# Adding a step's outputs onto its queries' products in PSUM, in a fused DeltaNet and feed-forward kernel

## The chip, the cores and the metric

The kernel runs on one core of a Trainium2 chip. The metric is the device time of one execution in microseconds. Before the change it is 647.7 us, the median of three runs (647.32, 647.70 and 648.19).

Engine names in the profile: PE is TensorE's matmuls and PEld its weight loads, DVE is VectorE, ACT is ScalarE, POOL is GpSimd, and SP is SyncE, which issues most of the DMAs. PSUM is the memory that TensorE writes to. Here it is used as eight banks of 512 floats in each of 128 partitions.

## The reference, cut to what matters

Two blocks follow each other. The first is a delta rule over 768 tokens, for 4 batches of 8 heads of 48 dimensions:

```python
for t in range(S):
    y[:, :, t] = einsum('bhd,bhde->bhe', q[:, :, t], state)
    v_old = einsum('bhde,bhd->bhe', state, kt)
    state = state + bt * einsum('bhd,bhe->bhde', kt, vt - v_old)
```

Its output, 3072 tokens of 384 features, goes through a feed-forward network (FFN): `h = x @ w_in` (2048 wide), `g = max(h, 0) + alpha * min(h, 0)`, `g @ w_out`.

## The kernel before, in words

**Chunks and steps.** The tokens are cut into 12 chunks of 64. A chunk is worked on in two steps, one for each pair of batches, so there are 24 steps (0 to 23), and step n works on the state of pair n mod 2. Inside a step the recurrence is written as matrix products, always for 16 heads, as `quarters()` (L482) lists them. Each of them is a small matmul on a quarter of the array (64 x 64 cells), and shows as two matmuls in the profile:

- `grams` (L495): products of the keys with each other, needed eight or nine steps ahead. VectorE weighs and moves them out in two pieces (`same` and `right`, L507); a third piece, `keep` (L544), copies a part on.
- `through_state` (L790): keys times the state and keys times the queries. VectorE subtracts the first from the values (`r`, L809) and masks the second into `a_t` (L521).
- `solve` (L821): the inverse of the chunk's triangular matrix times `r`. VectorE weighs it into `u` (L828).
- `query` (L778): queries times the state, the share of the output that comes from earlier chunks. ScalarE copies it to `y` (L788).
- `outputs` (L833): `a_t` times `u`, the share from the chunk itself. VectorE adds it to `y` (L843).
- `next_state` (L847): keys times `u`. VectorE subtracts it from the state (L861).
- `between` (L749): 32 x 32 blocks of the inverse of the next steps, copied out by ScalarE (L745).

`to_ffn` (L869) transposes `y` on TensorE; ScalarE copies that to `xt`, the FFN's input. `turn_q` (L462) is a stream transpose of the raw queries on VectorE (L466). It writes them beside the state of their pair, in the place that `query` and `through_state` of that step read, and step n + 2 uses the same place. `load_q` (L175) loads the raw queries on SP's queue, into two buffers in turn.

**Order.** All engines follow the order of the program text, which is written by hand; the framework only adds the semaphores. From step 6 (`JOINED`) a step is three stretches (L1856 to L1898). A stretch begins with a piece of attention on TensorE and goes on with 8 to 18 parts of the FFN of earlier chunks, among which the `later` pieces, the elimination on VectorE (`eliminate`) and the placing of blocks on ScalarE are woven in equal distances (`weave`, L1328).

1. `burst_a(n)` (L1374): `outputs` and `next_state` of step n - 1, `through_state` of step n, and at once all that moves them out.
2. `turn_round(n)` (L1411): `to_ffn` of step n - 1, then as later pieces the transposes of keys and queries for steps to come (`turn_q(n + 2)`), the weights, and `load_q(n + 3)`.
3. `burst_b(n)` (L1395): `solve(n)`, `grams(n + 9)`, `query(n + 1)` from step 8 on (`NARROW`), and `between`. The moving out of all of these follows in the order u, block copies, y, Gram products. From step 16 (`LATE`) only u is moved out at once, and the rest later in the stretch. Gram products end with step 14.

**PSUM.** Up to step 7 there are three pairs of banks for attention and two single banks for the FFN; from step 8 on two pairs and four single ones (`banks(2, 2)`, L1858). `ps_big()` (L77) hands out the pairs in turn. In `burst_b` the solve and the blocks lie in one pair (`b`), the Gram products and the queries' products in the other (`x`): per bank 256 columns of the one and 192 of the other. In `burst_a` outputs and the state's products lie in one pair and `through_state` in the other.

**The FFN.** Up to chunk 7 `ffn_in` (L957; L966 matmuls, L976 on ScalarE and L978 on VectorE) and `ffn_out_fast` (L1019; L1031 matmuls) work chunk by chunk. The latter multiplies in a scheme of seven products that needs sums of operands, which VectorE makes just before (`operand_sums`, L920). From chunk 8 on `ffn_in_fast` (L1153) and `ffn_out_faster` (L1258; L1283 matmuls) run. There ScalarE copies one bank (L1218), GpSimd adds in SBUF (L1223), VectorE adds another bank (L1228) and applies the slope (L1237); the times of these are due times counted in parts (`Due`, L1119).

Of the kernel before, what the change touches and what calls it, by code (L numbers as in the profile page):

```python
# [32 lines left out]
C = 64  # L33
# [3 lines left out]
EARLY = 8  # L37
FIRST = 6
NARROW = 8
# [5 lines left out]
def kernel(  # L45
# [20 lines left out]
    G = H // 2  # L66
# [10 lines left out]
    def ps_big():  # L77

        big.append(big.pop(0))
        return big[-1]  # L80
# [24 lines left out]
    def half(i):  # L105
        return slice(64 * i, 64 * i + 64)

    def dims(i):
        return slice(64 * i, 64 * i + D)
# [5 lines left out]
    N = len(steps)  # L115
# [240 lines left out]
    state = [x[:, :, :, 0:D] for x in beside]  # L356
# [15 lines left out]
    stats, k_t, q_t, a_t = {}, {}, {}, {}  # L372
# [112 lines left out]
    def now(pieces):  # L485
        for x in pieces:
            x()
# [7 lines left out]
    def grams(n, p=None):  # L495

        if n >= N:
            return []
        p = region(p, G * C, g=G)
        for g, a, t in quarters():  # L500
            nc.tensor.matmul(
                p[half(t), a, g], k_t[n][dims(a), g, half(t)], k_t[n][dims(a), g, half(t)]
            )

        def weighted(dst, cols):
            w = stats[n][1][:, 0:2, :, None].to_broadcast([128, 2, G, HB])
            nc.vector.tensor_tensor(  # L507
                out=dst.rearrange("p (a g) i -> p a g i", a=2), in0=p[:, :, :, cols], in1=w,
                op=ALU.mult,
            )  # L510

        return [
            lambda: weighted(gather(n), slice(0, HB)),
            lambda: weighted(right[n % EARLY][:, 1:], slice(HB, C)),
            lambda: keep(n),
        ]
# [251 lines left out]
    nv, rhs_, ys, us, xts, whole = {}, {}, {}, {}, {}, set()  # L768
# [9 lines left out]
    def query(n, p=None):  # L778
        if n >= N:
            return []  # L780
        bp = steps[n][1]
        p = region(p, G * D, g=G)
        for g, a, t in quarters():
            nc.tensor.matmul(
                p[half(t), a, g], q_t[n][dims(a), t, g], state[bp][dims(a), t, g]
            )
        ys[n] = work.tile([128, H, D], FP32, name="y")
        return [lambda: nc.scalar.copy(by_parity(ys[n]), p)]  # L788

# [31 lines left out]
    def solve(n, p=None):  # L821
        p = region(p, G * D, g=G)
        for g, a, t in quarters():
            nc.tensor.matmul(  # L824
                p[half(t ^ a), a, g], inv[n % NE][half(t), a * G + g], rhs_[n][half(t), a, g]
            )
        us[n] = work.tile([128, 2, G, D], FP32, name="u")
        return [lambda: nc.vector.tensor_tensor(  # L828
            out=us[n], in0=p,
            in1=stats[n][1][:, 0:3:2, :, None].to_broadcast([128, 2, G, D]), op=ALU.mult,  # L830
        )]

    def outputs(n, p=None):  # L833
        c, bp = steps[n]
        p = region(p, G * D, g=G)
        for g, a, t in quarters():
            nc.tensor.matmul(  # L837
                p[half(t), a, g], a_t[n][half(t ^ a), a * G + g], us[n][half(t ^ a), a, g]
            )
        if c == 0:  # L840
            ys[n] = work.tile([128, H, D], FP32, name="y")
            return [lambda: nc.scalar.copy(by_parity(ys[n]), p)]
        return [lambda: nc.vector.tensor_tensor(  # L843
            out=by_parity(ys[n]), in0=by_parity(ys[n]), in1=p, op=ALU.add
        )]

    def next_state(n, p=None):  # L847
        c, bp = steps[n]
        pieces, wide = [], n < 2 * NJ
        if c < NCH - 1:  # L850
            p = region(p, G * D, g=G)
            for g, a, t in quarters():
                nc.tensor.matmul(
                    p[half(a) if wide else dims(a), t, g], k_late[n % NKL][half(t ^ a), 2 * g + a, 0 : C if wide else D],
                    us[n][half(t ^ a), a, g],
                )


            def less(rows):
                x = state[bp][rows]  # L860
                nc.vector.tensor_tensor(out=x, in0=x, in1=p[rows], op=ALU.subtract)  # L861

            if wide:
                pieces = [lambda: less(slice(0, 2 * C))]
            else:
                pieces = [lambda: less(dims(0)), lambda: less(dims(1))]
        return pieces
# [503 lines left out]

    WY, JOINED = G * D, NJ + 2

    def burst_a(n):  # L1374

        soon, later = [], []
        b = ps_big()
        if n > JOINED:
            soon += outputs(n - 1, b[:, :, 0:WY])
            soon += next_state(n - 1, b[:, :, WY : 2 * WY])  # L1380
            later.append(lambda: load_late(n + 1))
        if n < N:
            p = ps_big()
            y = ps_big()[:, :, 0:WY] if n < NARROW else None
            soon += through_state(n, p[:, :, 0 : G * (D + C)], y)
            if n < JOINED + 2:
                soon += between_1(n + 1, b[:, :, 2 * WY : 2 * WY + G * HB])
            if n == JOINED:
                soon += grams(n + EARLY, big[-1][:, :, WY : WY + G * C])
                later.append(lambda: squares(n + EARLY + 1))  # L1390
            later.append(lambda: load_v(n + 3))
        now(soon)
        return later

    def burst_b(n):  # L1395

        b, x = ps_big(), ps_big()
        soon = solve(n, b[:, :, 0:WY])
        gram = grams(n + EARLY + 1, x[:, :, 0 : G * C])
        asked = query(n + 1, x[:, :, G * C : G * C + WY]) if n + 1 >= NARROW else []  # L1400
        wanted = [(n + 1, True, b[:, :, WY : WY + G * HB])]
        if n > JOINED:
            wanted.append((n + 2, False, b[:, :, 2 * WY : 2 * WY + G * HB]))
        soon += between(*wanted)
        if n >= LATE:
            now(soon[:1])
            return soon[1:] + asked
        now(soon + asked + gram[:2])
        return gram[2:] + [lambda: squares(n + EARLY + 2), lambda: load_early(n + EARLY + 3)]

    def turn_round(n):  # L1411

        if n > JOINED:
            to_ffn(n - 1)
        if n == JOINED:
            flips(n + EARLY + 1, N)
            load_keys(steps[TURNED_K][0])
        later = []
        if TURNED_K <= n + EARLY + 1 < N:
            later.append(lambda: turn_k(n + EARLY + 1))  # L1420
        if n + 2 < N:
            later.append(lambda: turn_q(n + 2))
        later += weigh(n + EARLY + 1)
        return later + [lambda: load_q(n + 3)]
# [120 lines left out]
    n = 2 * W_IN_P  # L1545
# [111 lines left out]
    n = 12  # L1657
# [198 lines left out]
    for n in range(JOINED, N):  # L1856
        if n == NARROW:
            banks(2, 2)  # L1858
        fill, share = FILL.get(n, FILLS[n % 2]), PIECES_OF.get(n, TURNS[n % NJ])
        extra = [[], [], []]  # L1860
        if n == JOINED:
            place(n + 1, (0,))
            extra[1] = [(weight_sums(1, 0, 3), 3)]
            extra[2] = [(weight_sums(0, 3, 4), 1)]
        elif n == JOINED + 1:
            extra[0] = [(weight_sums(1, 3, 4), 1, 0.6), (placing(n + 1, (1, 2, 3)), PLACING)]

        later = burst_a(n)
        stretch(fill[0], blocks, share[0], later, *extra[0], *put_off)
        put_off = []  # L1870
        later = turn_round(n)
        if n == JOINED:
            extra[1].append((placing(n + 1, (1, 2, 3)), PLACING))
        stretch(fill[1], blocks, share[1], later, *extra[1], soon=0.2)
        m, ends = (n + 6) // NJ, n % NJ == 2
        if ends and n > JOINED:
            for _ in blocks:
                assert False
            place(n + 2, (0,))
        later = burst_b(n) + [lambda: scale_v(n + 1)]  # L1880
        if n == JOINED:
            stretch(fill[2], blocks, share[2], later, *extra[2])
            for _ in blocks:
                assert False
            place(n + 2, (0,))
            place(n + 3, (0,))
            blocks = eliminate(m)
        else:
            if ends:
                blocks = eliminate(m) if m < N // NJ else iter(())  # L1890
            after = [(placing(n + 2, (1, 2, 3)), PLACING)]
            if n % NJ != 1:
                after.append((placing(n + 3, (0,)), 1))
            if n >= LATE:
                put_off, after = after, []
            stretch(
                fill[2], blocks, share[2], later, *after, *extra[2], soon=0.1 if n >= LATE else 0.5
            )  # L1898
# [34 lines left out]
```

## Time and profile before

| | us |
|---|---|
| median of three runs | 647.7 |
| the profiled execution, in all | 647.16 |
| its span, first to last instruction | 645.4 |
| PE busy | 630.1 |
| VectorE busy | 502.9 |
| ScalarE busy | 253.0 |
| GpSimd busy | 94.0 |

Below is the time of each engine from about one burst B to the next, six times: from those of steps 9 and 10, of steps 16 and 17, and of steps 20 and 21 on. Each row gives the length, then the busy time of PE, PEld, VectorE, ScalarE and GpSimd, each with its count of instructions, and then the granted clock of TensorE, the share of DMA and its rate in GB/s.

```profile
253.00:279.00 26.00, 25.60 (x384) 24.39 (x383) 21.22 (x56) 6.17 (x17) 0.74 (x4) 1.00 0.20 37
279.00:302.00 23.00, 23.00 (x345) 19.82 (x343) 17.89 (x44) 9.80 (x24) 2.11 (x5) 1.00 0.42 65
...
424.00:446.00 22.00, 22.00 (x311) 19.17 (x307) 18.60 (x47) 7.90 (x18) 0.00 (x0) 1.00 0.27 40
446.00:471.00 25.00, 25.00 (x359) 24.16 (x357) 22.68 (x53) 4.62 (x12) 0.00 (x0) 1.00 0.14 30
...
517.00:538.00 21.00, 21.00 (x354) 19.83 (x353) 16.47 (x28) 11.61 (x25) 12.57 (x22) 1.00 0.16 26
538.00:563.00 25.00, 25.00 (x360) 24.27 (x359) 16.06 (x35) 5.22 (x14) 1.40 (x3) 1.00 0.10 21
```

A row of the timeline has the start in us, the length, the engine, the line, the operation, what it writes and reads, shape, and count; in square brackets stands how long the engine was idle before it, and what ended that. A row of the chain of waits has the start, the length, and the engine with its tile and line. A row of the wait view has who waited for whom, the total in us, how often, and the longest.

### The profile page before, as it was taken

What the parts mean: (1) busy time and instruction counts of PE and PEld (TensorE: products, weight loads), DVE (VectorE), ACT (ScalarE), POOL (GpSimd) and SP (SyncE); (2) the same over time, 40 slices, a digit from 0 to 9 for tenths busy, and PEclk for the clock granted to TensorE, in tenths of its full rate; (3) what the DMA queues carried; (4) which work ended last, traced back from release to release, by engine and by line L of the source; (5) the groups of instructions that cost most, each with busy time, mean ns of one, the idle gap of its engine ahead of it and who ended that gap; (6) DMA issues with size and microseconds to landing.
All of it is one profiled execution on the core that took longest, in us unless ns stands there. A gap on an engine that the chain in (4) does not pass through costs nothing.

```text
span 645.4 us, 21564 instructions
## 1 busy us (share of the span) xinstructions
PE 630.1 (98%) x9199; PEld 556.2 (86%) x9199; DVE 502.9 (78%) x1206; ACT 253.0 (39%) x599; POOL 94.0 (15%) x204
## 2 busy tenths in 40 slices
PE   5999999999999999999999999999999999999997
PEld 4678888557778988988988988988999999999997
DVE  3986988977999879768979869769879569477383
ACT  5978565344453342243242243133145054041240
POOL 6001211010000000001000000000044053062360
PEclk9999999999999999999999999999999999999999
DMA  8967725211353243242242122122121220100000
GB/s 122 296 136 170 232 60 153 62 38 35 52 79 51 39 65 51 38 67 48 39 76 39 25 46 32 26 47 30 32 51 20 42 36 2 39 1 3 26 0 25
DMA packets 145968, 39.26 MB, mean 61 GB/s; under 512 B 139040, under 2 KB 142256, under 8 KB 145872
## 3 DMA queue, kind: packets, MB, share of 16 engines
q1 hardware_dynamic: 144000, 37.40, 28.4%
q8 instruction: 72, 1.18, 0.8%
q10 hardware_dynamic: 1872, 0.49, 0.4%
q14 instruction: 24, 0.20, 0.1%
HBM read 33.14 MB, written 4.72 MB: 59 GB/s over the span
## 4 chain that ended last, share of the span: by engine, by line
PE 77%; DVE 13%; ACT 5%; issue 2%; DMA 2%; SPq 1%; POOL 1%; DVEq 0%; POOLq 0%; ACTq 0%
PE p_ffn L966 12%; PE p_more L1283 8%; PE p_more L1031 7%; PE p_ffn L1031 7%; PE p_more L966 7%; PE p_ffn L1009 5%; PE p_more L1199 5%; PE p_ffn L1189 3%; PE p_ffn L1283 3%; PE p_ffn L1194 2%; DVE block L599 2%; PE p_pair L799 2%; PE p_pair L837 2%; PE p_pair L824 2%; PE p_pair L733 2%
## 5 line engine op out<-in xcount | busy, mean ns | idle before, releaser
L966 PE MATMUL p_ffn<-xt,w_in 128*128 128x256 f32 x528 | 123.1, 384 | 1.8 <-DVE act L978 1.8
L966 PEld LDWEIGHTS p_ffn<-xt,w_in 128*128 128x128 f32 x528 | 97.5, 190 | 16.0 <-ACT wgt L718 1.6
L966 PE MATMUL p_more<-xt,w_in 128*128 128x256 f32 x240 | 54.8, 381 | 0.0
L599 DVE TENSOR_TENSOR block<-block,prod 128x30 f32<-128x30 f32 (+9 forms) x150 | 49.8, 332 | 5.2
L1223 POOL TENSOR_TENSOR k_t<-k_t 128x128 f32<-128x128 f32 (+1 forms) x48 | 29.6, 616 | 163.7 <-ACT k_t L1218 161.2
L878 ACT COPY xt<-p_pair 128x384 f32<-128x384 f32 x22 | 10.4, 479 | 107.5 <-PE p_pair L876 107.3
L966 PEld LDWEIGHTS p_more<-xt,w_in 128*128 128x128 f32 x240 | 45.0, 190 | 6.3
L593 DVE TENSOR_TENSOR prod<-block 128x30 f32<-128x30 f32 (+9 forms) x150 | 48.8, 325 | 1.5
L418 POOL TENSOR_TENSOR beta_t<-beta_t,rec 128x8 f32<-128x8 f32 x24 | 5.9, 245 | 280.0 <-DVE rec L412 270.4
L976 ACT ACTIVATE act<-p_ffn 128x512 f32<-128x512 f32 x36 | 21.4, 593 | 53.1 <-PE p_ffn L966 53.0
L978 DVE SCALAR_TENSOR_TENSOR act<-act,al_t,p_ffn 128x256 f32<-128x256 f32 x72 | 30.9, 471 | 8.7 <-ACT act L976 8.6
L1223 POOL TENSOR_TENSOR block<-block 128x128 f32<-128x128 f32 (+1 forms) x48 | 28.0, 583 | 15.8 <-ACT block L1218 13.3
L1189 PE MATMUL p_ffn<-xt,w_in 128*128 128x256 f32 x96 | 28.7, 380 | 0.0
L1031 PE MATMUL p_ffn<-w_out,act 128*128 128x192 f32 x160 | 27.9, 330 | 0.0
L507 DVE TENSOR_TENSOR same<-p_pair,wgt 128x256 f32<-128x256 f32 x24 | 10.1, 422 | 22.3 <-ACT y L788 17.0
L745 ACT COPY inv<-p_pair 32x256 f32<-32x256 f32 x40 | 14.5, 362 | 33.1 <-DVE u L828 32.3
L976 ACT ACTIVATE act<-p_more 128x512 f32<-128x512 f32 x20 | 11.9, 595 | 37.2 <-PE p_more L966 37.2
L1031 PEld LDWEIGHTS p_ffn<-w_out,act 128*128 128x128 f32 x160 | 25.9, 190 | 0.4
L809 DVE TENSOR_TENSOR r<-v_raw,p_pair 64x192 f32<-64x192 f32 (+1 forms) x66 | 23.3, 352 | 2.3 <-PE p_pair L799 1.2
L828 DVE TENSOR_TENSOR u<-p_pair,wgt 128x384 f32<-128x384 f32 x24 | 13.2, 554 | 14.4 <-PE p_pair L733 13.6
L1031 PE MATMUL p_more<-w_out,act 128*128 128x192 f32 x128 | 22.2, 328 | 0.0
L1009 PE MATMUL p_ffn<-w_out,act 128*128 128x384 f32 x64 | 21.7, 490 | 0.2 <-ACT w_out L262 0.2
(252 smaller groups left out, 1489.5 us busy)
## 6 DMA issues: line engine op xcount, KB each, us to landing
w_out<-in_moe_w_in_dram SPq DMA_DIRECT2D x10, 512.0 KB, 5.6
v_raw<-in_v_dram SPq DMA_DIRECT2D x48, 96.0 KB, 2.8
kl<-in_k_dram SPq DMA_DIRECT2D x96, 48.0 KB, 2.5
out_dram<-o_sb SPq DMA_DIRECT2D x90, 48.0 KB, 1.6
space_out<-in_moe_w_out_dram SPq DMA_DIRECT2D x11, 384.0 KB, 4.3
ke_last<-in_k_dram SPq DMA_DIRECT2D x25, 96.0 KB, 3.1
qp<-in_q_dram SPq DMA_DIRECT2D x64, 32.0 KB, 2.2
w_out<-in_moe_w_out_dram SPq DMA_DIRECT2D x5, 384.0 KB, 4.5
```

Source lines behind the costliest of these rows:

```text
L593: nc.vector.tensor_tensor(out=prod, in0=r[:, 0:j, j : j + 1].to_broadcast([128, j, n]), in1=r[:, j : j + 1, j + 1 : HB].to_broadcast([128, ...
L599: nc.vector.tensor_tensor(out=r[:, 0:j, j + 1 : HB], in0=r[:, 0:j, j + 1 : HB], in1=prod, op=ALU.add)
L809: nc.vector.tensor_tensor(out=r[to, a], in0=v_in[to, a], in1=p[own, a, :, 0:D], op=ALU.subtract)
L966: nc.tensor.matmul(p_h[:, i], w_in[:, t, (f + i) * 128 : (f + i + 1) * 128], xt[:, t], start=(t == 0), stop=(t == KT - 1),)
L976: nc.scalar.activation(g, p_h, ACT.Relu, scale=-1.0)
L978: nc.vector.scalar_tensor_tensor(out=g[:, i], in0=g[:, i], scalar=al_t[:, f + i : f + i + 1], in1=p_h[:, i], op0=ALU.mult, op1=ALU.add,)
L1009: nc.tensor.matmul(p_o[u], gs[f // 2][:, f % 2, u * 128 : (u + 1) * 128], w_out[:, f], start=(f == 0), stop=(f == FT - 1),)
L1031: nc.tensor.matmul(p, x(i), w(i), start=(i == 0), stop=(i == FP - 1))
L1189: nc.tensor.matmul(p[:, f * 256 : f * 256 + 256], w(2, f), xt[:, 2], start=True, stop=False)
L1199: nc.tensor.matmul(q[:, j], a, b, start=True, stop=True)
L1223: nc.gpsimd.tensor_tensor(out=dst, in0=a, in1=b, op=ALU.add)
L1283: nc.tensor.matmul(p, x(i), w(i), start=(i == 0), stop=(i == FP - 1))
```

## The change: outputs accumulate onto the queries' products

From step 8 on `query` is computed in its own step's burst B, `query(n)` in place of `query(n + 1)`, after the Gram products and ahead of the solve. It is not copied out. Its pair of banks (`x`) is kept, on the list `asked_in`, until the next burst A. There `outputs` of the same step accumulates onto it: its matmuls do not start a sum but continue the one that `query` began. Only then ScalarE copies the whole sum to `y`. `next_state` writes to the columns of the same pair where the Gram products were.

Since `query(n)` now reads the transposed queries until burst B of step n, the transpose for step n + 2, which overwrites them, moves from the second stretch of the step to the third. Its load of raw queries stays where it was.

```diff
@@ query
             nc.tensor.matmul(
-                p[half(t), a, g], q_t[n][dims(a), t, g], state[bp][dims(a), t, g]
+                p[half(t), a, g], q_t[n][dims(a), t, g], state[bp][dims(a), t, g],
+                start=(n < NARROW or g == 0), stop=(n < NARROW),
             )
+        if n >= NARROW:
+            return []
@@ outputs
             nc.tensor.matmul(
-                p[half(t), a, g], a_t[n][half(t ^ a), a * G + g], us[n][half(t ^ a), a, g]
+                p[half(t), a, g], a_t[n][half(t ^ a), a * G + g], us[n][half(t ^ a), a, g],
+                start=(n < NARROW), stop=(n < NARROW or g == G - 1),
             )
-        if c == 0:
+        if c == 0 or n >= NARROW:
@@ burst_a
-        b = ps_big()
+        if n > NARROW:
+            b = asked_in.pop()
+            y, z = b[:, :, G * C : G * C + WY], b[:, :, 0:WY]
+        else:
+            b = ps_big()
+            y, z = b[:, :, 0:WY], b[:, :, WY : 2 * WY]
         if n > JOINED:
-            soon += outputs(n - 1, b[:, :, 0:WY])
-            soon += next_state(n - 1, b[:, :, WY : 2 * WY])
+            soon += outputs(n - 1, y)
+            soon += next_state(n - 1, z)
@@ burst_b
         b, x = ps_big(), ps_big()
+        gram = grams(n + EARLY + 1, x[:, :, 0 : G * C])
+        if n >= NARROW:
+            asked_in.append(x)
+            query(n, x[:, :, G * C : G * C + WY])
         soon = solve(n, b[:, :, 0:WY])
-        gram = grams(n + EARLY + 1, x[:, :, 0 : G * C])
-        asked = query(n + 1, x[:, :, G * C : G * C + WY]) if n + 1 >= NARROW else []
...
         if n >= LATE:
             now(soon[:1])
-            return soon[1:] + asked
-        now(soon + asked + gram[:2])
+            return soon[1:]
+        now(soon + gram[:2])
@@ turn_round
-        if n + 2 < N:
+        if n < NARROW:
             later.append(lambda: turn_q(n + 2))
@@ the loop over steps, third stretch
         later = burst_b(n) + [lambda: scale_v(n + 1)]
+        if NARROW <= n < N - 2:
+            later.append(lambda: turn_q(n + 2))
```

## The prediction

> **What bounds the kernel now.** I read the busy table and its slices first, then TensorE's waits cut to the part the change can reach, then the chain of waits around the one wait found, then the timeline of single bursts.
>
> ```profile
> PE 630.1 (98%) x9199; PEld 556.2 (86%) x9199; DVE 502.9 (78%) x1206; ACT 253.0 (39%) x599; POOL 94.0 (15%) x204
> PE   5999999999999999999999999999999999999997
> ```
>
> TensorE is busy in 98% of the span, and in every slice but the first and last at 90% or more. The granted clock is 0.999, so nothing is to be had there. Which microseconds can the change touch? The stream transposes of queries (L466, sixteen of them, 182.5 to 532.9 us) mark the steps: they belong to steps 6 to 21. So the second burst of step 7, the first that loses something, starts at 208 us. From 218 us to the end the wait view of TensorE has one line:
>
> ```profile
> PE p_more L1031 <- DVE sums L920: 0.4, 1, 0.4
> ```
>
> Busy time alone would be weak proof, since matmul ends are modelled. The Trainium skill says so too (Trainium Kernel Development and Optimization, Best Practices): matmul busy time is a poor measure of how near a kernel is to its limit, so the 98% could hide slack that a freed VectorE would return. Therefore I look at starts. In the chain of waits, sixteen matmuls of the second FFN product (L1031, later L1283) take 2.60 us wherever they follow their like, at 272 us as at 637, and twelve of the first (L966) 2.59: 163 and 216 ns each, without a spread. A TensorE that waited for buffers would show uneven pieces. So from 218 us on TensorE is the limit, and other engines count only where they make it wait.
>
> That one wait, in the chain of waits:
>
> ```profile
> 257.79 0.48 DVE u L828
> ...
> 258.29 0.36 ACT inv L745
> ...
> 259.41 0.37 ACT mid L745
> ...
> 259.80 0.49 ACT y L788
> ...
> 260.38 0.42 DVE same L507
> 260.81 0.33 DVE right L507
> 261.14 0.61 DVE sums L920
> ...
> 261.77 0.70 DVE sums L920
> ...
> 262.52 1.57 PE p_more L1031 x8
> ```
>
> Read it upwards: the matmuls waited for operand sums, these for the two Gram evictions (same, right), and these for ScalarE's copy of the queries' products y, which stands behind four block copies, which wait for VectorE's own u. VectorE waits here for something that waited for VectorE. The wait view of VectorE shows how often:
>
> ```profile
> DVE same L507 <- ACT y L788: 17.0, 8, 2.1
> ```
>
> Eight times 2.1 us: the second bursts of steps 7 to 14, those with both a query and a Gram product. The Gram products and the queries' products lie in the same banks.
>
> **The change, part by part.**
>
> *Removed: VectorE's addition.* Sixteen L843 additions of 0.55 us (steps 8 to 23), 8.8 us of VectorE. It lies beside TensorE. Value on the path: nothing by itself.
>
> *Removed: the wait of same for y.* In burst B there is no y copy any more, so same and right can follow u: 2.1 us of VectorE for each of the eight. At step 9 this decides: u ends at 258.25, and with 2.1 us less the second operand sum ends near 260.4 rather than 262.46. The eight L1031 before it start at 260.66 and need 8 x 0.163 = 1.30 us, so the next is due at 261.96; it started at 262.52. That is **0.56 us** of TensorE to be gained, and the sums would then have 1.6 us in hand. What is late next there? Nothing in the wait view.
>
> *Moved: ScalarE's copy.* Sixteen copies of 0.48 us before, sixteen after; they go from burst B to burst A, where they take the addition's place, in front of the copy of the FFN's banks. ScalarE is busy 39% and sat idle 2.57 us before its first work after such a burst (L1218 at 480.88). Cost nothing, covered by that idle time. Without it the limit is the copy L1218 itself, whose bank TensorE needs again 0.70 to 0.75 us after it ends (481.47 to 482.21, for instance).
>
> *Added: a wait.* The state's products now lie in y's banks, as the Gram products do today, and same waits for y today. So the state's subtraction (L861) will wait for ScalarE's copy instead of following the addition on its own engine. Queued behind it on VectorE are three r subtractions, the mask of a_t and the next FFN total (L1228). At step 18: state products start at 478.43 and take 0.36, the copy can run from about 479.0 to 479.5, and VectorE reached L861 at 479.89. So it is free in time. If the copy waits for the whole burst (end 479.7), L861 starts at about 480.2, 0.3 later than now. What would that hurt?
>
> ```profile
> 483.55 0.59 ACT L1218 COPY k_t<-p_more 128x512 f32<-128x512 f32 x1 [1.16 <-DVE act L1228]
> ```
>
> This copy waited for L1228, and ends 0.83 us before TensorE needs the bank (next group at 484.96). So VectorE may be up to 0.8 us late here before TensorE stalls. I take 0, with bounds of -0.5 us of VectorE time and +0.3. The Trainium skill (PSUM — Partial Sum Buffer, PSUM bank collisions raise a hardware error) says that two engines on one bank and quadrant must be kept apart, even two readers in different columns. The trace agrees: same and y read different columns of one bank, and same waited 2.13 us. By that rule the new wait is certain; its price is the sum above.
>
> *Moved: the transposes.* From step 8 on L466 (0.71 us) goes one stretch later, past burst B, with its query loads still issued at their old place by SP. Each load now finds its buffer freed one stretch later, but still about a stretch ahead; the products read the transposed queries a step later. Everything VectorE does between the old and the new place comes 0.7 us earlier, everything after is level, unless VectorE was idle between; then it is up to 0.7 later. In steps 9 to 14 the lost 2.1 us wait outweighs it. At 18, 20 and 22 there is idle time after burst B (VectorE waited 2.25 us before 476.61); the scaling of v moves into it, the transposes take its place (0.71 for 0.5), and the addition that follows is gone (-0.5): level or earlier. Value 0; bounds -0.7 and +0.2 us of VectorE, neither of which reaches TensorE past the 0.8 in hand.
>
> *Turned round: burst B on TensorE.* The same matmuls, in the order Gram, query, solve, between instead of solve, Gram, query, between. From the timeline of TensorE, start to start:
>
> ```profile
> 375.95 0.68 PE L824 MATMUL p_pair<-r,inv 64*64 64x48 f32 x32
> ...
> 376.46 0.66 PE L501 MATMUL p_pair<-k_t 48*64 48x64 f32 x32
> ...
> 376.94 0.63 PE L784 MATMUL p_pair<-beside 48*64 48x48 f32 x32
> ...
> 377.50 0.22 PE L733 MATMUL p_pair<-inv,mid 32*32 32x32 f32 x2
> ```
>
> Solve 0.51, Gram 0.48, query 0.56 up to the 32x32 blocks. The very last solve goes straight to another tile size, and there takes 0.61:
>
> ```profile
> 584.08 0.68 PE L824 MATMUL p_pair<-r,inv 64*64 64x48 f32 x32
> 584.70 1.08 PE L1283 MATMUL p_more<-w_out,act 128*128 128x192 f32 x5
> ```
>
> So a change of tile size costs about 0.11, and query alone is 0.45. New: 0.48 + 0.45 + 0.61 = 1.54, against 1.55. Steps 15 and later have no Gram: 0.45 + 0.61 = 1.06 against 1.08. Step 7 loses a query, step 23 gains one. Together 0. Not in the trace: the step from query (48 rows) to solve (64 rows). Its nearest rows are solve to Gram (64 to 48, no extra) and a change of tile size (0.11); I take the nearer, 0, because both use tiles of 64 x 64. Bounds 0 to 16 x 0.11 = 1.8 us. The Trainium skill (TensorEngine Tiling (Array Packing), Key Properties) says that changing the tiling mode drains TensorE, not changing tiles within it; by that rule the term is 0 as well. A product that accumulates costs no more than one that doesn't: L1031 has 0.163 us for the first and for later ones of a sum.
>
> **The sum.** The profiled execution took 647.16 us, 645.4 of it span and 1.8 around it. Less 0.56: 646.6. The median of the runs is 647.7, 0.54 above that execution; on its scale the forecast is **647.1 us**. Times within 0.2% (1.3 us) count as the same, about what a measurement of this kernel can tell from no change.
>
> **The rivals.**
> 1. *The stall stays.* same waits for something else, or the sums stay late because of the slopes before them: 647.7. For it: those slopes end at 257.8 only. Against: then the sums still have 1.6 us. Chance 12%.
> 2. *Burst B gets longer* (the other side): query to solve costs as a change of tile size, 16 x 0.11 = 1.8, less 0.56: 648.9; without the gain 649.5. From 0.12 a step it is over 1.3 us net of the gain. For it: no row has that order. Against: solve to Gram at 0.50. Chance 9%.
> 3. *VectorE comes late after burst A.* The copy stands behind two placing copies (0.50 and 0.39) as well as the whole burst: L861 at about 481.1, 1.2 late, 0.4 beyond the 0.8 in hand, in three steps (18, 20, 22): 648.3; in all sixteen 653. Against: the copy is issued before these. Chance 8%, most of it slower.
> 4. *TensorE hides slack*, and some of the 17 + 8.8 us that VectorE gains reaches the end: a tenth of it gives 645.1. Against: the even pieces. Chance 11%.
>
> Forecast 60%. Faster: rival 4, 12% with a little of the forecast. Slower: rivals 2 and most of 3, 15%. Same: 73%. The range takes in half of rival 4 and rival 2 with its gain: 645.8 to 649.0.
>
> **What would show it.** Right: no wait of same for y; no gap before L1031 at 262; L843 from step 8 gone; L788's copies in burst A, L861 waiting for them; burst B 1.54 from its first start to the 32x32 blocks. Wrong: a TensorE wait after 218 us on L1218 or L861's followers, solve over 0.61 us after the query, or a span that moves by over a microsecond while these starts are even.

## The result, and the profile after

The changed kernel is slower: 650.2 us, the median of 20 executions (649.16 to 653.2), against 647.38 us (646.05 to 651.14) for 20 of the kernel before in the same comparison. The ratio is 1.0048, with a 95% interval of 1.0036 to 1.0059. The forecast was 647.1 us and no change, with a range from 645.8 to 649.0. The profiled execution took 650.66 us, 648.9 of it span. Line numbers below are those of the kernel whose trace is shown; in the changed kernel they are three or four higher than before (the solve L824 is now L827, the FFN's L966 and L1031 are L970 and L1035).

The busy table of the kernel after:

```profile
PE 630.6 (97%) x9199; PEld 556.3 (86%) x9199; DVE 495.9 (76%) x1190; ACT 254.4 (39%) x599; POOL 92.3 (14%) x204
```

VectorE has 16 instructions and 7.0 us less. TensorE has as many matmuls and nearly the same busy time (630.1 before), but the span is 3.5 us longer: most of the time is lost in gaps, not in longer work. The wait view of TensorE in the kernel after, from 205 us to the end, has one line:

```profile
PE p_pair L733 <- issue: 2.5, 2, 1.3
```

Two gaps, and the releaser is "issue": TensorE waited for no engine and no transfer that the profile shows. The chain of waits of the kernel after, from 350 us, shows where the first one lies (start, length, what):

```profile
350.64 0.62 PE p_pair L501 x32
351.27 0.45 PE p_pair L784 x32
351.72 0.47 PE p_pair L827 x32
352.19 0.65 PE p_pair L733 x48
352.84 1.29 issue
354.12 0.25 PE p_pair L733 x3
354.37 2.15 PE p_more L1035 x12
```

This is burst B of step 13: Gram products, queries, solve, and the 32 x 32 blocks of `between`. TensorE stops three matmuls before the end of the blocks, inside one piece of work whose operands are there, and goes on 1.29 us later. The other gap lies at the same place in step 14. From start to start the two take 1.48 us (352.63 to 354.12) and 1.40 us (379.64 to 381.04); beside a gap, blocks follow each other in 0.01 to 0.02.

**What TensorE waits for is its own instructions.** They come to it by DMA. The list of DMA queues of the kernel after has (packets, MB, share):

```profile
q8 instruction: 72, 1.18, 0.8%
```

72 packets of 16,384 bytes; TensorE has 9199 loads, 9199 matmuls and 97 instructions of its sequencer, 257 for each packet, so the text takes a packet as 256 instructions of 64 bytes. The two gaps come after TensorE's instructions number 10,944 and 11,712. Both leave 192 when divided by 256. Where a block really begins is not in the trace: the count starts at its first TensorE instruction, and "block end" below means a multiple of 256 in this count. In the trace a packet of instructions began at 351.79 and one at 378.77 (0.95 and 0.93 us long), and TensorE went on 2.33 and 2.28 us after these starts. A burst B with a Gram product has 320 instructions in about 2.2 us, 7 ns each, so it uses up a block of 256 in 1.8 us; the FFN's instructions come at about 108 ns each and a block lasts 28 us. The Trainium skill (Runtime: NRT & Kernel Launch, Instruction fetch mechanics) has the same block of 256 instructions, the next one fetched while the current one runs, and calls the cost mostly hidden. The trace agrees on the block, and in these two bursts disagrees on the hiding.

What the change has to do with it: it moves one query, 32 matmuls with their loads or 64 instructions, from step 7 to step 8 and so on, each to the next step. From there to step 23 every burst B stands 64 instructions earlier against the blocks of 256. The table has the place of the block end in burst B, in instructions from the burst's start:

| step | 8 | 9 | 10 | 11 | 12 | 13 | 14 |
|---|---|---|---|---|---|---|---|
| before | 77 | 156 | 156 | 235 | 235 | 58 | 58 |
| after | 141 | 220 | 220 | 43 | 43 | **122** | **122** |

At 122 the next 192 instructions all lie in the burst, and the gap comes behind them, at 314 of 320. The same could be said of 58, which gave no gap; the last section shows what tells the two apart.

The kernel before had shown it as well, early in the span. The wait view of TensorE in the kernel before, over the whole span, has these lines (at 79 and 43 us; also behind a remainder of 192 or 193, and ended 2.3 to 2.4 us after a packet's start):

```profile
PE p_pair L501 <- issue: 0.7, 1, 0.7
PE p_pair L853 <- issue: 0.5, 1, 0.5
```

The kernel after has a third line of this kind early in the span, at 50 us and behind the same remainder:

```profile
PE p_pair L669 <- issue: 0.9, 1, 0.9
```

The kernel before has no gap there, though TensorE's instructions up to that place are the same. So the place alone does not fix whether, and how long, TensorE waits; it also differs from one execution to the next.

### The profile page after: what moved, and what is told of

The parts are those of the page before. It is cut to its first block, busy times and chain, and to the rows that moved or that the text cites. A ratio compares the mean times of both kernels' runs of the same rounds, so it can differ in the third digit from the quotient of the medians.

```text
span 648.9 us, 21553 instructions
## 1 busy us (share of the span) xinstructions
PE 630.6 (97%) x9199; PEld 556.3 (86%) x9199; DVE 495.9 (76%) x1190; ACT 254.4 (39%) x599; POOL 92.3 (14%) x204
## 4 chain that ended last, share of the span: by engine, by line
PE 84%; DVE 5%; DMA 5%; SPq 2%; ACT 2%; issue 2%; ACTq 0%; DVEq 0%
PE p_ffn L970 12%; PE p_ffn L1035 9%; PE p_more L1287 8%; PE p_more L970 8%; PE p_more L1035 8%; PE p_ffn L1013 7%; PE p_more L1203 5%; PE p_ffn L1193 3%; PE p_ffn L1287 3%; PE p_ffn L1198 2%; DMA ke_pair<-in_k_dram 2%; PE p_pair L733 2%; PE p_pair L802 2%; PE p_pair L840 2%; PE p_pair L827 2%; PE p_pair L678 2%
## 5 line engine op out<-in xcount | busy, mean ns | idle before, releaser
L970 PE MATMUL p_ffn<-xt,w_in 128*128 128x256 f32 x528 | 123.5, 384 | 2.1 <-DVE act L982 1.8
L970 PEld LDWEIGHTS p_ffn<-xt,w_in 128*128 128x128 f32 x528 | 97.3, 190 | 16.9 <-ACT wgt L718 1.6
L970 PE MATMUL p_more<-xt,w_in 128*128 128x256 f32 x240 | 54.8, 381 | 0.0
L970 PEld LDWEIGHTS p_more<-xt,w_in 128*128 128x128 f32 x240 | 45.0, 190 | 6.2
L1035 PE MATMUL p_ffn<-w_out,act 128*128 128x192 f32 x160 | 27.9, 330 | 0.0
L1035 PEld LDWEIGHTS p_ffn<-w_out,act 128*128 128x128 f32 x160 | 25.9, 190 | 0.4
L982 DVE SCALAR_TENSOR_TENSOR act<-act,al_t,p_more 128x256 f32<-128x256 f32 x40 | 17.3, 473 | 8.5 <-ACT act L980 8.4
L1241 DVE SCALAR_TENSOR_TENSOR act<-block,al_t,act 128x256 f32<-128x256 f32 x32 | 20.1, 667 | 4.7 <-ACT block L1237 4.6
L846 ACT COPY y<-p_pair 128x384 f32<-128x384 f32 x18 | 8.6, 476 | 37.8 <-PE p_pair L857 32.2
```

The costliest lines, as they stand in the source:

```text
L970: nc.tensor.matmul(p_h[:, i], w_in[:, t, (f + i) * 128 : (f + i + 1) * 128], xt[:, t], start=(t == 0), stop=(t == KT - 1),)
L982: nc.vector.scalar_tensor_tensor(out=g[:, i], in0=g[:, i], scalar=al_t[:, f + i : f + i + 1], in1=p_h[:, i], op0=ALU.mult, op1=ALU.add,)
L1035: nc.tensor.matmul(p, x(i), w(i), start=(i == 0), stop=(i == FP - 1))
```

## The experiments

The padding in six of them is a function that multiplies two constant pieces into a bank from which nobody reads the products; each of its matmuls uses a quarter of the array, shows as two in the profile, and so gives four instructions on TensorE, loads counted. It shifts all that follows and takes its own time (16 of them start from 224.6 to 225.1 us in pad16). It takes its bank where the kernel takes one anyway, so the banks go on being handed out in the same order. The times of the kernel before are those of the same chip and comparison.

**pad16: the old place against the blocks again.** The kernel after, with 64 instructions put in before burst B of step 8, ahead of the transposes of `to_ffn`.

```diff
+    def pad(count, p):
+        p = region(p, G * D, g=G)
+        for i in range(count):
+            g, a, t = quarters()[i % 16]
+            nc.tensor.matmul(p[half(t), a, g], ident[dims(a), half(t)], ident[dims(a), 0:D])
...
-        if n > JOINED:
+        if n == NARROW:
+            p = ps_big()
+            pad(16, p[:, :, 0 : G * D])
+            to_ffn(n - 1, p[:, 0])
+        elif n > JOINED:
             to_ffn(n - 1)
```

> The changed kernel with 16 small matmuls more (64 TensorE instructions), of constants, unread, ahead of the transposes of step 8. They put back what step 7 lost when its query product moved to step 8, so that every later instruction stands again at the count it had in the kernel before. Theory of instruction supply (TensorE runs out of instructions in the bursts of steps 13 and 14, because a block of 256 ends at the wrong place there; 1.3 us of idle time each in the trace of the changed kernel): both gaps go, no other comes, 2.8 us gained, 0.45 us paid for the 16; time 647.9, within 0.2% of the kernel before, and the gap at 262 us of the kernel before (0.56 us) is absent too. Rival, the banks held until the next burst A or ScalarE's copy in a new place make TensorE wait: both gaps stay, 650.7. Rival, the order Gram, query, solve makes the blocks wait for their operands: both gaps stay, 650.7.

Measured: 647.48 us against 647.96, ratio 0.9994 (0.9979 to 1.0009). More work, and the loss is gone. TensorE has no wait at all after 205 us. The busy time by stretch shows it: steps 13 and 14 in the kernel after,

```profile
350.00:376.00 26.00, 24.71 (x380) 23.64 (x380) 18.97 (x50) 6.37 (x17) 0.72 (x4) 1.00 0.12 25
376.00:398.00 22.00, 20.79 (x334) 17.95 (x333) 14.54 (x32) 8.36 (x20) 1.54 (x3) 1.00 0.27 45
```

and in pad16:

```profile
350.00:376.00 26.00, 26.00 (x392) 24.60 (x394) 19.86 (x50) 6.38 (x18) 0.66 (x4) 1.00 0.15 30
376.00:398.00 22.00, 22.00 (x341) 19.36 (x342) 15.98 (x38) 8.94 (x21) 1.42 (x2) 1.00 0.27 40
```

Behind the limits of the stretch a row has its length, then TensorE's busy time: 1.29 and 1.21 us are missing after, none in pad16, and nothing of the change has been taken back.

**pad24: another shift.** As pad16 with `pad(24, ...)`, 96 instructions.

> The same with 24 small matmuls, 96 instructions. Theory of instruction supply: counted by the ends of the blocks of 256, the bursts of steps 13 and 14 are safe, and those of steps 9 and 10 now hold a whole block: gaps of about 1.4 us each in the bursts B of steps 9 and 10, near 254 and 280 us, and none at 13 and 14; time 647.9 + 2.7 + 0.2 = 650.8. Rival, held banks or late engines: gaps at 13 and 14 as in the changed kernel and none at 9 and 10; 650.9. So the time is the same by both, and the place tells them apart.

Measured: 653.29 us against 647.96, ratio 1.0097 (1.006 to 1.0134). The timeline of TensorE in pad24 has the gaps in the bursts B of steps 9 and 10, and none in 13 and 14:

```profile
256.36 0.22 PE L733 MATMUL p_pair<-diag,right 32*32 32x32 f32 x2 [1.08 <-issue]
...
284.13 0.22 PE L733 MATMUL p_pair<-diag,right 32*32 32x32 f32 x2 [2.08 <-issue]
```

There the block end lies at 124. Where the gaps are follows the count of instructions. That eight matmuls more than pad16 make the kernel 5.8 us slower (2.5 more than was expected) is more than the two gaps of 3.2 us; a part of the rest is the clock, below.

**before_pad48: the kernel before, with none of the change.** The same function in the kernel before, `pad(48, ...)`, 192 instructions: 192 later is 64 earlier against blocks of 256.

> The kernel before, with 48 small matmuls (192 instructions) ahead of the transposes of step 8, so that from there on the instructions stand against the blocks of 256 as in the changed kernel (192 more is 64 less, modulo 256). Nothing of the change is in it. Theory of instruction supply: gaps of about 1.4 us in the bursts B of steps 13 and 14, and 1.35 us for the 48 matmuls: 647.4 + 2.8 + 1.35 = 651.5. Rival, the change's own waits are the cause: no gaps, 648.7.

Measured: 654.23 us against 647.96, ratio 1.009 (1.0071 to 1.011). The timeline of TensorE in before_pad48 has the gaps at the places of the changed kernel, steps 13 and 14:

```profile
357.02 0.25 PE L733 MATMUL p_pair<-diag,right 32*32 32x32 f32 x3 [1.74 <-issue]
...
386.01 0.25 PE L733 MATMUL p_pair<-diag,right 32*32 32x32 f32 x3 [1.60 <-issue]
```

This clears the accumulation, the held banks and the order Gram, query, solve: none is in this kernel. It too lost more than expected (651.5). TensorE's gap at 262 us for the operand sums is absent here as well, though nothing of the change is in the kernel and `same` waits for y eight times as before; TensorE comes to those products 3.2 us later than before, VectorE to the sums 2.6 us.

**move_only: the query in its own step, without the accumulation.** The kernel after, but `outputs` starts its own sums in a fresh pair, the query's products are copied to `y` in burst B, and VectorE adds.

```diff
-                start=(n < NARROW or g == 0), stop=(n < NARROW),
...
-            b = asked_in.pop()
...
+        b = ps_big()
...
+        asked = query(n, x[:, :, G * C : G * C + WY]) if n >= NARROW else []
...
-        now(soon + gram[:2])
+        now(soon + asked + gram[:2])
```

> The changed kernel without the accumulation: query products are computed in their own step after the Gram products, the transposes are late, but ScalarE copies the query products at once and VectorE adds the outputs to them, and no banks are held. TensorE has the same instructions in the same order. Theory of instruction supply: the gaps of steps 13 and 14 are there (2.8 us); VectorE's waits for the copy (2.1 us each) are back, and with them perhaps the gap of 0.56 us at 262 us: 650.2 to 650.8. Rival, the held banks or ScalarE's late copy cause the gaps: no gaps, 647.4 to 648.

Measured: 652.42 us against 647.96, ratio 1.0062 (1.0042 to 1.0083), again more than expected (650.2 to 650.8). The gaps are there, in steps 13 and 14 (1.30 and 1.61 us), so they need no accumulation and no held banks. VectorE's wait is back too, and no TensorE wait on the sums came with it, which bears on the gain (see "What held"). The wait view of VectorE in move_only:

```profile
DVE same L507 <- ACT y L788: 14.9, 7, 2.1
```

**early_pad: the shift in the first 30 us.** The kernel after; 18 padding matmuls (72 instructions) in place of two early fillers (8), 64 more in all.

```diff
-    for _ in range(6):
+    for _ in range(4):
         busy(0.25, mid[1])
+    for _ in range(2):
+        pad(9, ps_big()[:, :, 0 : G * D])
```

> The changed kernel with 64 TensorE instructions more in the first 30 us, where TensorE multiplies the unit matrix while it waits for VectorE: 18 small matmuls take the place of two larger ones there (72 instructions for 8). Theory of instruction supply: from there on all instructions stand 64 later against the blocks of 256, so the bursts of steps 13 and 14 hold no whole block and there is no gap after 205 us; the 16 are no longer paid for. What is left of the change is the gap of 0.56 us at 262 us that it takes away: 0.9991 of the kernel before, 646.9 beside 647.5; with the interval of such a comparison hardly to be told from it. Rival, any change to the code's length costs some microseconds by itself: slower than the kernel before by about 0.4%.

Measured: 646.48 us against 647.7, ratio 0.9979 (0.9967 to 0.9991). No TensorE wait after 205 us. It is faster than the kernel before by 1.2 us of the medians: the 0.56 us of the gap at 262 us, which is absent, and some 0.7 us more, whose source is open (two fillers are gone, and all the early bursts are shifted as well).

**pad8 and pad44: two more shifts, one execution each.** `pad(8, ...)`, 32 instructions, and `pad(44, ...)`, 176.

> The changed kernel with 8 small matmuls (32 instructions) ahead of the transposes of step 8. Theory of instruction supply, counted by the blocks of 256: one gap of about 1.3 us in the burst B of step 8, near 232 us, and none or a small one in those of steps 13 and 14. Rival, held banks: gaps at 13 and 14 alone.

> The changed kernel with 44 small matmuls (176 instructions) ahead of the transposes of step 8. Theory of instruction supply, counted by the blocks of 256: gaps of about 1.4 us in the bursts B of steps 11 and 12, near 304 and 330 us, and none at 8, 9, 10, 13, 14. Rival, held banks: gaps at 13 and 14 alone.

Measured: pad8 652.48 us, pad44 654.5, against 647.7. In pad8 one gap, of 1.91 us, at step 8, where the block end lies at 109; none in steps 13 and 14, where it lies at 90. In pad44 two, of 1.48 and 1.62 us, in steps 11 and 12, where it lies at 123. So far, a block end 109 to 124 instructions into the burst gives a gap of 1.1 to 2.1 us; at 141 it was 0 to 0.4 us; from 11 to 90 and from 156 on, none. One execution each says little of the sizes.

**split: the same shift, less dense.** The kernel after, nothing padded; in steps 13 and 14, four FFN parts of that stretch are put inside burst B, between query and solve.

```diff
+        if n in (13, 14):
+            for _ in range(4):
+                next(tail)
...
-                fill[2], blocks, share[2], later, *after, *extra[2], soon=0.1 if n >= LATE else 0.5
+                fill[2] - (4 if n in (13, 14) else 0), blocks, share[2], later, *after, *extra[2], soon=0.1 if n >= LATE else 0.5
```

> The changed kernel, nothing added or left out; in steps 13 and 14 alone, four parts of the feed-forward block that otherwise follow burst B stand inside it, between the query products and the solve. The count of TensorE instructions and the ends of the blocks of 256 are where they were, or at most 16 instructions off. Theory of instruction supply: a block of 256 now lasts 1.7 to 2.6 us longer there, which is more than the 1.35 us that were lacking, so both gaps go; two more changes of tile size in each cost 0.2 us; 650.2 - 2.8 + 0.4 = 647.8. Rival, it is not how fast the instructions of the block are used up but that the end of a block falls into a burst at all: both gaps stay, 650.6.

Measured: 648.54 us against 647.61, ratio 1.0006 (0.9992 to 1.002). Both gaps are gone. The wait view of TensorE in split, from 205 us on, has no L733:

```profile
PE p_ffn L970 <- DVE act L982: 1.4, 1, 1.4
PE p_ffn L970 <- issue: 0.4, 1, 0.4
```

(The two are at 205 us and in step 8.) So the block end alone does not cost: with the same count of instructions, four FFN parts inside the burst are enough to cover it. This fits a block that is used up faster than the next packet comes.

## Why the prediction was wrong

**The step that failed** is the last of its parts, "Turned round: burst B on TensorE", with "Step 7 loses a query, step 23 gains one. Together 0". Its times are right. From start to start burst B now takes 0.515 from Gram to query, 0.453 from query to solve and 0.577 from solve to the blocks, 1.545 against the 1.54 forecast. But it weighed matmuls by their time alone. That a query's 64 instructions go from step 7 to step 8 was counted as nothing, while it moves every burst B from step 8 to step 23 against the supply of instructions. In terms of the sum: 2.88 us for the two gaps from start to start, less 0.03 that the blocks would take anyway, is **2.85 us that stood at 0**.

With the gap of 0.56 us that is gone the net is +2.3. The measured difference of the medians is 2.8. The 20 executions of the kernel after tell where most of the rest may be: 13 had a mean granted clock of 1.000, and their median is 649.72, 2.3 above the 647.38 of before. Six had 0.997, and their median is 652.5; one had 0.995 and took 649.88. 0.003 of 648 us is 1.9 us, about what a stretch of 3.4 us at half clock costs (1.7). Where in the span these six lost their clock was not traced; five of the experiments show such a drop right after a gap (last section). The two profiled executions differ by 3.5. There the kernel after was also behind early: by 208 us, ahead of the first burst whose work is changed, TensorE had been busy 195.6 us against 196.5. That is the size of the third early gap, 0.9 us at 50 us.

**What held.** *The wait of same for y* is gone, and the gap at 262 us with it. VectorE in the timeline of the kernel after, at step 9:

```profile
257.13 0.55 DVE L831 TENSOR_TENSOR u<-p_pair,wgt 128x384 f32<-128x384 f32 x1
257.60 0.41 DVE L507 TENSOR_TENSOR same<-p_pair,wgt 128x256 f32<-128x256 f32 x1
```

`same` follows `u` at once. The products that had waited for the operand sums follow their like in 1.30 us (261.44 to 262.74), the 8 x 0.163 of the forecast, and the second sum ended at 259.67, 3.1 us ahead of them (1.6 were forecast).

That the gap went because the wait went is not shown, however. In move_only VectorE still waits at step 9, and TensorE has no gap. Its timelines, first of VectorE, then (the last two rows) of TensorE:

```profile
259.83 0.42 DVE L507 TENSOR_TENSOR same<-p_pair,wgt 128x256 f32<-128x256 f32 x1 [2.12 <-ACT y L788]
...
261.22 0.69 DVE L920 TENSOR_TENSOR sums<-sums,act 128x512 f32<-128x512 f32 x1
261.29 1.46 PE L1031 MATMUL p_more<-space_out,sums 128*128 128x192 f32 x8
262.59 1.46 PE L1031 MATMUL p_more<-more,sums 128*128 128x192 f32 x8
```

The second sum ends at 261.91, 0.68 us ahead of the products at 262.59. One cause is the moved transpose of queries (L466, 0.71 us), which stood at 253.16 before and stands at 241.66 here: from the first operand sum of step 9 at 248 us to the third, VectorE took 7.96 us before (248.36 to 256.32) and 7.25 here (248.53 to 255.78). TensorE also came to these products 0.63 us later. The prediction put the transposes at 0; by this they alone make up for more than the 0.56 us. So the amount was right, but which of the two parts gave it in the changed kernel stays open, and in that the prediction was lucky.

*The new wait* is there. The wait view of VectorE in the kernel after:

```profile
DVE beside L865 <- ACT y L846: 4.4, 7, 1.2
```

Seven times, at most 1.2 us. That is not lateness of as much: the addition of 0.55 us that stood ahead of L865 is gone. Whether VectorE was ever past the +0.3 of the bounds was not measured step by step; no TensorE wait followed. *Copy and transposes* cost nothing; no wait of TensorE for VectorE, ScalarE or a DMA is left after 205 us.

**The rivals.** The stall (1) did not stay. The order query, solve (2) costs nothing: 0.453 to the solve, where its price would have made it 0.56. A late VectorE (3) would be a TensorE wait with a VectorE releaser; there is none. And TensorE (4) shows no slack that 7 us less on VectorE returned: in pad16, where the gaps are away, the gain is within 0.2%. Only the 0.7 us of early_pad whose source is open leave room for some. The kernel is slower by a mechanism that none of the four names.

**Where it could have been read.** TensorE's waits were cut to 218 us and later, where the change works, and only one line was left. The lines with "issue" at 43 and 79 us were outside the cut, though the code there has the same bursts of small matmuls. A wait that nobody releases, behind a run of dense instructions, was the clue. Counting TensorE's instructions up to these two gaps would have given 1472 and 3009, remainders 192 and 193 of 256, and the table of block ends above could have been written from the kernel before and the diff. That would not have given a sure size, but a rival on the slower side: two bursts with the block end in their middle, at 0.5 to 0.7 us each by the early lines, 1.0 to 1.4 us in all.

## What to carry to other kernels

Where a kernel issues hundreds of small matmuls within a couple of microseconds, an edit that changes only how many instructions stand ahead of such bursts can move the time by some tenths of a per cent, in either direction, without any engine having to wait longer for another. So look for gaps with releaser "issue" and for their remainder by the size of an instruction packet before putting a loss down to the edit's idea, and test it with a few harmless instructions as padding, in the kernel before too. In split, larger matmuls inside the burst were enough with the block end at 122; a padding fits one version only and is lost with the next edit.

## What the runs showed of the hardware

**Running out of instructions.** TensorE's gaps come at a fixed place against blocks of 256 instructions (remainder 192 or 193 in all eleven gaps of over 1 us with releaser "issue" after 205 us) and end 2.3 to 2.7 us after an instruction packet starts. When that packet starts tells a block end at 109 from one at 90. In the eleven bursts of steps 8 to 14 with the block end at 109 to 124, all traces but split taken together, the packet began 1.0 to 2.0 us after the burst did. In the 24 with the block end at 90 or less, a packet had begun 1.2 to 7.9 us ahead of the burst, when TensorE was 55 to 104 instructions short of the block end, and no gap followed. With the block end at 156 or more the packet began inside the burst or behind it, but the 192 instructions behind the block end reach past the burst into the FFN's slower ones. Bursts of 256 instructions (from step 15 on) had no gap in these traces.

**Gaps of 1 to 2 us were often followed by half the clock.** The busy time by stretch in pad24, around the end of its second gap at 284.13 (the number behind the last count in brackets is the granted clock):

```profile
280.90:284.10 3.20, 1.15 (x98) 0.99 (x89) 0.48 (x2) 0.00 (x0) 0.00 (x0) 1.00 0.56 95
284.30:287.70 3.40, 3.40 (x10) 2.77 (x9) 1.79 (x4) 2.66 (x7) 0.00 (x0) 0.50 0.23 31
287.70:291.10 3.40, 3.40 (x17) 2.92 (x16) 1.46 (x3) 0.72 (x2) 0.00 (x0) 1.00 0.31 34
```

For 3.4 us the clock is 0.50, and TensorE does 10 matmuls where it does 17 in the next 3.4 us. The traces of before_pad48 (358.1 to 361.6), move_only (354.4 to 357.8), pad44 (308.6 to 312.0) and pad8 (237.2 to 240.6) have the same, each beginning 0.2 to 1.1 us after a gap ended; six of the eleven gaps were not followed by one, those of the kernel after among them. Apart from the last 2 us of a span, no trace has such a stretch after 205 us without a gap just ahead of it. Where it comes it costs about 1.7 us more, and is part of what pad24 and before_pad48 lost beyond their gaps. The Trainium skill (TensorE: Matmul & The Clock Gate, What's actually happening) lets the clock fall to half after an idle window of about 3.4 us. The length of the drop agrees with that window; the idle time does not: here it followed gaps of 1.3 to 2.1 us in a burst of small matmuls, though not all of them. What decides is open.
